# One more fold of the odd rows in a Fourier product: half the columns per product, two row tiles of 128 and 60 rows

## The chip, the cores and the metric

The kernel runs on one core of one Trainium2 chip. The metric is the device time of one launch in microseconds (us). The record lists every run as fast; the program runs on a single core, and no run stood out as slow. In this kernel SBUF holds the tiles that the engines read and write, and PSUM the results of the matmuls.

## The reference, cut to what matters

```python
def _attn_ref(x):                      # x: (8, 3008, 256) float32
    X = np.fft.fft(x, axis=1)          # over the sequence, S = 3008
    X = np.fft.fft(X, axis=2)          # over the features, D = 256
    return X.real.astype(np.float32)

def _moe_ref(x, w_in, w_out):          # w_in (256, 2048), w_out (2048, 256)
    h = x @ w_in
    r = np.maximum(h, 0.0)
    return (r * r @ w_out).astype(np.float32)
```

## The kernel before

TensorE does two things. The **main loop** multiplies the transformed sequence with the first weight (`front`, two products per half step) and the squared result with the second (`back`, seven products per step). The **transform over S** of sequence b + 1 is slipped between the half steps of sequence b as "side work", paced by weights. It is done with tables of cosines and sines. The input is folded first, by symmetry, so that only n from 0 to S/4 = 752 is left. The n are then cut into classes, each with its own small product, and VectorE joins the results. Class 3 holds the 376 odd n, and its products are the ones that the change replaces:

```python
def class_tiles(S):                     # rows (n) by class, at most 128 per tile
    half = S // 8 + 1
    tiles = []
    for c, order in enumerate((range(0, half, 4), range(2, half, 4), range(1, half, 2), range(half, S // 4 + 1))):
        for r in range(0, len(order), P):
            tiles.append((c, order[r], order.step, len(order[r:r + P])))
    return tiles                        # rows: 95 | 94 | 128, 60 | 128, 128, 120

            def product(ps, c):         # one product per row tile of the class
                ts = [t for t in range(NT) if TILES[t][0] == c]
                for t in ts:
                    ...
                    nc.tensor.matmul(ps, w, tab[0:rows, kp, PLACE[t]:PLACE[t] + NC[kp][c]],
                                     start=t == ts[0], stop=t == ts[-1])

            def even_n():               # classes 0, 1 (95 columns) and 2 (189 columns)
                ...
                for c, at, nk in ((0, 0, n2), (1, n2, n2), (2, 2 * n2, n1)):
                    product(st["ps"][:, at:at + nk], c)

            def odd_n():                # class 3, 377 or 376 columns
                st["odd"] = psd.tile([P, 512], F32, name="pd", tag="d")[0:n, 0:n0]
                product(st["odd"], 3)

            def join_1():               # VectorE: even and odd n together
                both(dst[...], dst[...], st["c"], st["odd"])

    def between():                      # called after each half step of the main loop
        nonlocal spent
        if i < 2 * NJ:                  # NJ = 8 steps make one block
            return
        spent -= pace
        while side and spent <= 0:
            t, f = side.pop(0)
            f()
            spent += t
```

There is one such group (even product, odd product, joins) for each parity of k (`kp`) and for cosine and sine (`which`): four per sequence.

Of the kernel before, what the change touches and what calls it, by code (L numbers as in the profile page):

```python
# [8 lines left out]
F32 = mybir.dt.float32  # L9
U32 = mybir.dt.uint32  # L10
AF = mybir.ActivationFunctionType
ALU = mybir.AluOpType
PSUM = bass.MemoryType.PSUM
P = 128
R = 32



# [59 lines left out]
def kernel(  # L78
# [12 lines left out]
    nc = tc.nc  # L91
    B, NROW, _, D = x.shape
    S = out.shape[0] // B
    M = S // 2
    NKT = M + 1
# [14 lines left out]
    const = ctx.enter_context(tc.tile_pool(name="const", bufs=1))  # L110
    xp = ctx.enter_context(tc.tile_pool(name="xp", bufs=NX))
    fp = ctx.enter_context(tc.tile_pool(name="fp", bufs=2))
    wp = ctx.enter_context(tc.tile_pool(name="wp", bufs=NT))
    pq = ctx.enter_context(tc.tile_pool(name="pq", bufs=2))
    hp = ctx.enter_context(tc.tile_pool(name="hp", bufs=3))
    gp = ctx.enter_context(tc.tile_pool(name="gp", bufs=4))
# [11 lines left out]

    xt = {}

    def load_x(b, t):
        _, r0, step, rows = TILES[t]

        while rows % 15 and rows % 16 and r0 + step * rows < NROW:
            rows += 1

        pool, tag = (gp, "g") if b == 0 and t < NT - NX else (xp, "x")
        xt[b, t] = pool.tile([P, 4, D], F32, name="xt", tag=tag)
        nc.sync.dma_start(out=xt[b, t][0:rows], in_=x[b, r0:r0 + step * (rows - 1) + 1:step])
# [121 lines left out]

    folded = {}
    PQE = {}
    NE = B - 1
    xe, we = {}, {}
    e_dram = dp.tile([NE, NKT], F32, name="e_dram")
    e_rows = const.tile([NE, NKT], F32, name="e_rows")

    def load_column(t):

# [14 lines left out]
    def fold(b, t):  # L285


        r = slice(0, TILES[t][3])
        st = {}

        def new(pool, nm, shape):
            st[nm] = pool.tile(shape, F32, name=nm, tag=nm)
            return st[nm]

        def f_s():
            v = xt[b, t]
            tt(out=new(fp, "fs", [P, 2, D])[r], in0=v[r, 0::2], in1=v[r, 1::2], op=ALU.add)

        def f_d():
            v = xt[b, t]  # L300
            tt(out=new(fp, "fd", [P, 2, D])[r], in0=v[r, 0::2], in1=v[r, 1::2], op=ALU.subtract)  # L301
            if b > 0 and b * NT + t + NX < B * NT:
                load_x(*divmod(b * NT + t + NX, NT))

        def f_sc():
            s, sc = st["fs"], new(fp, "sc", [P, 2, H + 1])
            nc.vector.tensor_copy(sc[r, :, 0:H + 1:H], s[r, :, 0:H + 1:H])
            tt(out=sc[r, :, 1:H], in0=s[r, :, 1:H], in1=s[r, :, D - 1:H:-1], op=ALU.add)

        def f_dc():  # L310
            d = st["fd"]
            tt(out=new(fp, "dc", [P, 2, H - 1])[r], in0=d[r, :, 1:H], in1=d[r, :, D - 1:H:-1], op=ALU.subtract)

        def f_p():
            sc, wP = st["sc"], new(wp, "wP", [P, 2, H + 1])
            for kp in range(2):
                tt(out=wP[r, kp], in0=sc[r, 0], in1=sc[r, 1], op=ALU.subtract if kp else ALU.add)
            folded[b, t, 0] = wP

        def f_q():  # L320
            dc, wQ = st["dc"], new(wp, "wQ", [P, 2, H - 1])
            for kp in range(2):
                tt(out=wQ[r, kp], in0=dc[r, 0], in1=dc[r, 1], op=ALU.add if kp else ALU.subtract)
            folded[b, t, 1] = wQ

        return [(0.7, f_s), (0.7, f_d), (0.5, f_sc), (0.4, f_dc), (0.6, f_p), (0.6, f_q)]

    def dft_ops(b):



        def start():
            PQE[b] = [pq.tile([n, NKT], F32, name=nm, tag=nm)
                      for nm, n in (("Pt", P), ("Qt", P - 1), ("Et", P))]

        def group(kp, which):
            n = NE if b is None else P - 1 if which == 1 else P
            tab = sinT if which == 1 else cosT
            n2, _, n1, n0 = NC[kp]
            st = {}  # L340

            def product(ps, c):
                ts = [t for t in range(NT) if TILES[t][0] == c]
                for t in ts:
                    rows = TILES[t][3]
                    w = we[t] if b is None else folded[b, t, which % 2]
                    w = w[0:rows, kp]
                    w = w[:, H:H + 1].to_broadcast([rows, n]) if which == 2 and b is not None else w[:, 0:n]
                    nc.tensor.matmul(ps, w, tab[0:rows, kp, PLACE[t]:PLACE[t] + NC[kp][c]],  # L349
                                     start=t == ts[0], stop=t == ts[-1])  # L350

            def even_n():
                st["ps"] = psd.tile([P, 512], F32, name="pd", tag="d")[0:n]
                a = st["a"] = hp.tile([P, 2 * P], F32, name="da", tag="da", bufs=2)[0:n]
                for c, at, nk in ((0, 0, n2), (1, n2, n2), (2, 2 * n2, n1)):
                    product(st["ps"][:, at:at + nk], c)
                nc.scalar.copy(a[:, 0:n2], st["ps"][:, 0:n2])

            def both(lo, hi, a, ps):

                nk, nh = a.shape[-1], hi.shape[-1]
                tt(out=lo, in0=a, in1=ps, op=ALU.add)  # L362
                if which == 1:
                    tt(out=hi[:, ::-1], in0=ps[:, 0:nh], in1=a[:, 0:nh], op=ALU.subtract)
                else:
                    tt(out=hi[:, ::-1], in0=a[:, 0:nh], in1=ps[:, 0:nh], op=ALU.subtract)

            def join_4():
                a, ps = st["a"], st["ps"]
                st["b"] = hp.tile([P, 2 * P], F32, name="db", tag="db", bufs=2)[0:n, 0:n1]  # L370
                both(st["b"][:, 0:n2], st["b"][:, n2:n1], a[:, 0:n2], ps[:, n2:2 * n2])

            def join_2():
                a, ps = st["b"], st["ps"]
                st["c"] = hp.tile([P, NC[0][3]], F32, name="dc2", tag="dc2", bufs=2)[0:n, 0:n0]
                both(st["c"][:, 0:n1], st["c"][:, n1:n0], a, ps[:, 2 * n2:2 * n2 + n1])

            def odd_n():
                st["odd"] = psd.tile([P, 512], F32, name="pd", tag="d")[0:n, 0:n0]
                product(st["odd"], 3)  # L380

            def join_1():
                dst = e_rows if b is None else PQE[b][which]
                nh = S // 8
                both(dst[:, kp:kp + 2 * n0 - 1:2], dst[:, M - kp - 2 * (nh - 1):M - kp + 1:2], st["c"],
                     st["odd"])

            return [(0.5, even_n), (0.5, join_4), (0.7, join_2), (0.0, odd_n), (1.2, join_1)]

        ops = [] if b is None else [(0.0, start)]  # L390
        for which in (2,) if b is None else (0, 1) if b else (0, 2, 1):
            for kp in range(2):
                ops += group(kp, which)
        if b is None:
            ops.append((0.0, lambda: nc.sync.dma_start(out=e_dram[:, :], in_=e_rows)))
        return ops

    def load_e(b):
# [203 lines left out]
    def between():  # L602

        nonlocal spent
        if i < 2 * NJ:
            return
        spent -= pace
        while side and spent <= 0:
            t, f = side.pop(0)
            f()  # L610
            spent += t

    flight, finished = [], []
    for i in range(len(steps) + LAG + 4):
        if i < len(steps):
            b, k0, n, j = steps[i]
            if i == NJ:
                for t in range(NX):
                    load_x(1, t)
            if NJ <= i < NJ + NT:  # L620
                load_column(i - NJ)
            if i % per == 0:
                assert not side
                side = ahead(b + 1) if b + 1 < B else []
                spent, pace = 0.0, sum(t for t, _ in side) / (2 * (per - (0 if i else 2 * NJ)) - 6)
            g = front(b, k0, n, j, between)
            if i < NJ:
                s = combine(n, g, True)
            elif i < 2 * NJ:
                sum_wout(j)  # L630
        while finished and finished[0][0] <= i:
            store(*finished.pop(0)[1:])
        if i >= LAG and flight:
            at, g_, s_ = flight.pop(0)
            final = at[:3] == (B - 1, *BLOCKS[-1])
            back(at[2], at[3], g_, s_, final)
            if at[3] == NJ - 1:
                c_ = gather(at[2], s_ is None, final)
                finished += [(i + 2 + s, *at[:3], s, c_, final) for s in range(2)]
        for f in products:  # L640
            f()
        products = [next_weight() for _ in range(2 if i + 2 < NJ else 1 if i < NJ else 0)]
        if i < len(steps):
            flight.append(((b, k0, n, j), g, s if i < NJ else combine(n, g, False)))
# [63 lines left out]
```

## Time and profile before

| | before |
|---|---|
| median of 3 runs | 1997.95 us (1997.23 to 2001.38) |
| TensorE busy | 98% of the span |
| VectorE, ScalarE, GpSimd busy | 70%, 45%, 58% |
| odd products of sequences 1 to 7 | 28 x 1.90 us |
| even products of sequences 1 to 7 | 28 x 1.37 us, each with a visit to 60-row weights |

The prediction below shows the lines. In them a matmul in fp32 is two records, PE is the matmul and PEld the weight load, which normally hides under the matmul before it.

### The profile page before, as it was taken

To read this page: it belongs to the slowest core of one execution; us is meant where nothing else is said; L and a number is where in the kernel's file an instruction comes from. 1 tells how busy PE (TensorE), PEld (TensorE's weight loads), DVE (VectorE), ACT (ScalarE), POOL (GpSimd) and SP (SyncE) were. 2 spreads that over 40 slices of the span, in tenths; PEclk is the share of its full clock that TensorE was granted. 3 is DMA by queue.
4 is the path that set the end of the run, shared out by engine and by line. 5 is a ranking of instruction groups with operands and counts; after the bars stand their busy time and mean duration, and the time that the engine had idled before them with its cause. 6 is when DMAs were issued, how large, how long until landed. Compare 5 with 4: busy or idle time off the path is not lost.

```text
span 1999.2 us, 27284 instructions
## 1 busy us (share of the span) xinstructions
PE 1963.1 (98%) x9104; PEld 1704.3 (85%) x9104; DVE 1392.0 (70%) x3492; ACT 897.6 (45%) x973; POOL 1159.3 (58%) x1695
## 2 busy tenths in 40 slices
PE   6899999999999999999999999999999999999998
PEld 3688888888888888888888888888888888888887
DVE  7788866777568765777558875687657776555554
ACT  1654444444444444444445444444444454445443
POOL 0026645666566755676556665666656675566664
PEclk8899999999999999999999999999999999999999
DMA  6232101110011111111011110111001100100100
GB/s 183 95 57 50 38 11 32 47 32 22 11 52 32 27 27 32 26 39 40 11 27 37 39 30 11 31 42 37 21 11 43 41 11 16 31 11 11 22 11 21
DMA packets 144687, 68.49 MB, mean 34 GB/s; under 512 B 128440, under 2 KB 135547, under 8 KB 144546
## 3 DMA queue, kind: packets, MB, share of 16 engines
q1 hardware_dynamic: 143470, 66.24, 14.3%
q8 instruction: 71, 1.16, 0.2%
q10 hardware_dynamic: 1076, 0.52, 0.1%
q14 instruction: 70, 0.57, 0.1%
HBM read 42.03 MB, written 24.68 MB: 33 GB/s over the span
## 4 chain that ended last, share of the span: by engine, by line
PE 94%; DVE 3%; ACT 1%; DMA 1%; issue 0%; SPq 0%; DVEq 0%; ACTq 0%
PE ph L412 16%; PE ph L413 16%; PE mA L465 16%; PE mC L465 16%; PE mB L465 16%; PE mD L465 8%; PE pd L349 5%; DMA xt<-in_x_dram 1%; DVE he L415 0%; PE mA L452 0%; PE mB L452 0%; DVE g L418 0%; PE pg L236 0%; DVE fd L301 0%; ACT g L427 0%
## 5 line engine op out<-in xcount | busy, mean ns | idle before, releaser
L427 ACT ACTIVATE g<-g 128x1004 f32<-128x1004 f32 (+1 forms) x384 | 400.1, 1042 | 896.6 <-DVE g L418 503.6
L415 DVE SCALAR_TENSOR_TENSOR he<-Et,gE,ph 128x251 f32<-128x251 f32 (+1 forms) x768 | 361.8, 471 | 474.9 <-PE ph L413 473.3
L435 POOL TENSOR_TENSOR s<-g 128x251 f32<-128x251 f32 (+1 forms) x376 | 248.6, 661 | 746.5 <-ACT g L428 690.9
L412 PE MATMUL ph<-Pt,G 128*128 128x251 f32 (+1 forms) x1536 | 454.5, 377 | 3.5 <-ACT G L237 2.5
L413 PE MATMUL ph<-Qt,G 127*128 127x251 f32 (+1 forms) x1536 | 452.3, 375 | 0.0
L428 ACT ACTIVATE g<-g 128x1004 f32<-128x1004 f32 (+1 forms) x384 | 399.9, 1041 | 12.2
L465 PE MATMUL mC<-s,wsum 128*128 128x251 f32 (+1 forms) x1504 | 381.3, 374 | 0.0
L465 PE MATMUL mA<-g,wout 128*128 128x251 f32 (+1 forms) x1504 | 380.9, 375 | 0.0
L417 DVE TENSOR_TENSOR g<-he,ph 128x251 f32<-128x251 f32 (+1 forms) x768 | 320.6, 417 | 55.6 <-POOL s L437 0.5
L412 PEld LDWEIGHTS ph<-Pt,G 128*128 128x128 f32 x1536 | 288.0, 189 | 48.0 <-issue 4.5
L413 PEld LDWEIGHTS ph<-Qt,G 127*128 127x128 f32 x1536 | 291.7, 190 | 36.5 <-DVE Qt L362 0.5
L465 PEld LDWEIGHTS mA<-g,wout 128*128 128x128 f32 x1504 | 282.5, 189 | 41.6 <-issue 2.9
L465 PEld LDWEIGHTS mC<-s,wsum 128*128 128x128 f32 x1504 | 285.5, 190 | 34.5
L418 DVE TENSOR_TENSOR g<-he,ph 128x251 f32<-128x251 f32 (+1 forms) x768 | 314.2, 409 | 0.0
L436 POOL TENSOR_TENSOR s<-s,g 128x251 f32<-128x251 f32 (+1 forms) x376 | 282.1, 750 | 29.4
L437 POOL TENSOR_TENSOR s<-g 128x251 f32<-128x251 f32 (+1 forms) x376 | 290.3, 772 | 0.0
L438 POOL TENSOR_TENSOR s<-g,s 128x251 f32<-128x251 f32 (+1 forms) x376 | 247.9, 659 | 0.0
L465 PE MATMUL mB<-g,wsum 128*128 128x251 f32 (+1 forms) x752 | 220.4, 374 | 0.0
L465 PE MATMUL mD<-s,wout 128*128 128x251 f32 (+1 forms) x752 | 220.3, 374 | 0.0
L465 PE MATMUL mB<-s,wout 128*128 128x251 f32 (+1 forms) x752 | 219.9, 374 | 0.0
L465 PEld LDWEIGHTS mB<-g,wsum 128*128 128x128 f32 x752 | 142.6, 190 | 17.4
L465 PEld LDWEIGHTS mD<-s,wout 128*128 128x128 f32 x752 | 141.9, 189 | 17.7
(85 smaller groups left out, 1271.0 us busy)
## 6 DMA issues: line engine op xcount, KB each, us to landing
out_dram<-os SPq DMA_DIRECT2D x376, 56.0 KB
xt<-in_x_dram SPq DMA_DIRECT2D x24, 512.0 KB
xt<-in_x_dram SPq DMA_DIRECT2D x16, 384.0 KB
Et<-e_dram SPq DMA_DIRECT2D x7, 752.5 KB
out_dram<-os SPq DMA_DIRECT2D x288, 6.8 KB
raw<-in_moe_w_in_dram SPq DMA_DIRECT2D x16, 256.0 KB
raw<-in_moe_w_out_dram SPq DMA_DIRECT2D x16, 256.0 KB
xt<-in_x_dram SPq DMA_DIRECT2D x8, 480.0 KB
```

The costliest lines, as they stand in the source:

```text
L412: nc.tensor.matmul(hP, G1[:, fs], pt[:, ks], start=True, stop=True)
L413: nc.tensor.matmul(hQ, G2[:, fs], qt[:, ks], start=True, stop=True)
L415: nc.vector.scalar_tensor_tensor(out=t, in0=et[:, ks], scalar=gE[:, fc:fc + 1], in1=hP, op0=ALU.mult, op1=ALU.add)
L417: tt(out=g[:, h, 0, 0:n], in0=t, in1=hQ, op=ALU.add)
L418: tt(out=g[:, h, 1, 0:n][:, ::-1], in0=t, in1=hQ, op=ALU.subtract)
L427: act(v, v, AF.Relu)
L428: act(v, v, AF.Square)
L435: gt(out=s1, in0=g21, in1=g22, op=ALU.add)
L436: gt(out=s2, in0=s1, in1=g11, op=ALU.subtract)
L437: gt(out=s3, in0=g11, in1=g21, op=ALU.subtract)
L438: gt(out=s4, in0=g12, in1=s2, op=ALU.subtract)
L465: nc.tensor.matmul(acc[nm][:, i, 0:n], w, v[:, 0:n], start=j == 0 and i == 0, stop=j == NJ - 1, skip_group_check=True)
```

## The change

The intent is to halve the columns of the odd products. The odd n from 1 to 751 pair up as n and 752 - n. For even k the sum and the difference of a pair suffice; for odd k a rotation turns the pair into a cosine and a sine transform on the even-k table. So 188 rows are left in place of 376, and each product needs 189 columns instead of 377. In exchange there are two parts per product, and VectorE and ScalarE have to reverse, add and rotate the rows. The core of the diff:

```diff
+    ODD0 = NT - 3
+    HALF = S // 16                      # 188
+    REST = HALF - P                     # 60
...
+        def f_turn():                   # VectorE: reverse the second half of the rows
+            ...
+                nc.vector.stream_shuffle(w, w, REVERSE)
+            nc.scalar.copy(st["f0"][rows], st["v"][rows, 0])
+        def f_even():
+            tt(out=v, in0=a, in1=w, op=ALU.add)
+            tt(out=w, in0=a, in1=w, op=ALU.subtract)
+            sine(spare("f1", "f1"), st["w"], (0, 1))      # ScalarE, two scalings each
+            sine(spare("f2", "f0"), st["v"], (1, 0))
+        def f_odd():
+            ... nc.vector.scalar_tensor_tensor(out=u, in0=u, scalar=turn[rows, 0, i:i + 1], in1=st[nm][rows], ...)
+        return ops + [(0.7, f_turn), (0.9, f_even), (1.0, f_odd)]
...
             def odd_n():
-                st["odd"] = psd.tile([P, 512], F32, name="pd", tag="d")[0:n, 0:n0]
-                product(st["odd"], 3)
+                ps = psd.tile([P, 512], F32, name="pd", tag="d")[0:n]
+                st["odd"] = ps[:, 0:n0]
+                if not b:
+                    return product(ps[:, 0:n0], 3)
+                nq = (n0 + 2) // 2 if kp else (n0 + 1) // 2
+                for part in range(2):
+                    if kp:
+                        tab, o = (cosT, sinT)[part], 0
+                        to = ps[:, part * nq:part * nq + nq]
+                    else:
+                        tab, o = (cosT, sinT)[which], part
+                        to = ps[:, part:n0:2]
+                    other = part != which
+                    for i, (rows, pair) in enumerate(((P, (ODD0, ODD0 + 1)), (REST, (ODD0 + 2, NT)))):
+                        at = PLACE[ODD0 + i]
+                        nc.tensor.matmul(to, folded[b, pair[other]][0:rows, kp, PART[which]][:, 0:n],
+                                         tab[0:rows, 0, at + o:at + NC[0][3]:2], start=i == 0, stop=i == 1)
+                if kp:                   # a ScalarE copy, then VectorE joins the two parts
+                    ...
...
     def between():
-        if i < 2 * NJ:
+        if i < NJ:
             return
-        spent -= pace
+        spent -= pace / 2 if i < 2 * NJ else pace
```

More of the change, by code (lines that the diff above doesn't have):

```diff
@@ L112 @@
     fp = ctx.enter_context(tc.tile_pool(name="fp", bufs=2))
-    wp = ctx.enter_context(tc.tile_pool(name="wp", bufs=NT))
+    wp = ctx.enter_context(tc.tile_pool(name="wp", bufs=NT + 1))
     pq = ctx.enter_context(tc.tile_pool(name="pq", bufs=2))
@@ L129 @@
     xt = {}
-    def load_x(b, t):
-        _, r0, step, rows = TILES[t]
+    ODD0 = NT - 3
+    HALF = S // 16
+    REST = HALF - P
+    ODD = [[(0, 0, P)],
+           [(p, 2 * HALF - p - R, R) for p in range(0, P, R)],
+           [(0, P, H // 2)] + [(H // 2 + p, 2 * HALF - P - p - R, R) for p in range(0, H // 2, R)]]
+    assert H == P and REST <= H // 2 and TILES[ODD0][0] == 3 and TILES[ODD0 + 1][1] == TILES[ODD0][1] + P
+    def load_x(b, t):
+        c, r0, step, rows = TILES[t]
+        if b and c == 3:
+            xt[b, t] = xp.tile([P, 4, D], F32, name="xt", tag="x")
+            for p, first, count in ODD[t - ODD0]:
+                nc.sync.dma_start(out=xt[b, t][p:p + count], in_=x[b, S // 8 + 1 + first:S // 8 + 1 + first + count])
+            return
         while rows % 15 and rows % 16 and r0 + step * rows < NROW:
@@ L263, with make_turn @@
     PQE = {}
+    PART = (slice(0, H + 1), slice(H + 1, D))
+    REVERSE = list(range(R - 1, -1, -1))
+    turn = const.tile([P, 3, 2], F32, name="turn")
+    def make_turn():
+        for i in range(2):
+            for a, tab in enumerate((cosT, sinT, sinT)):
+                nc.scalar.mul(turn[:, a, i:i + 1], tab[:, 1, PLACE[ODD0 + i]:PLACE[ODD0 + i] + 1], -1.0 if a == 2 else 1.0)
     NE = B - 1
@@ L266 @@
     e_dram = dp.tile([NE, NKT], F32, name="e_dram")
-    e_rows = const.tile([NE, NKT], F32, name="e_rows")
     def load_column(t):
@@ L285, in fold @@
     def fold(b, t):
-        r = slice(0, TILES[t][3])
+        odd = b > 0 and t >= ODD0
+        r = slice(0, P if odd else TILES[t][3])
         st = {}
@@ L312, in f_dc, with w_of @@
             tt(out=new(fp, "dc", [P, 2, H - 1])[r], in0=d[r, :, 1:H], in1=d[r, :, D - 1:H:-1], op=ALU.subtract)
+        def w_of(t):
+            if (b, t) not in folded:
+                folded[b, t] = wp.tile([P, 2, D], F32, name="w", tag="w")
+            return folded[b, t]
         def f_p():
-            sc, wP = st["sc"], new(wp, "wP", [P, 2, H + 1])
+            sc, w = st["sc"], w_of(t)
             for kp in range(2):
-                tt(out=wP[r, kp], in0=sc[r, 0], in1=sc[r, 1], op=ALU.subtract if kp else ALU.add)
@@ L318, in f_p @@
-            folded[b, t, 0] = wP
+                tt(out=w[r, kp, PART[0]], in0=sc[r, 0], in1=sc[r, 1], op=ALU.subtract if kp else ALU.add)
         def f_q():
-            dc, wQ = st["dc"], new(wp, "wQ", [P, 2, H - 1])
+            dc, w = st["dc"], w_of(t)
             for kp in range(2):
-                tt(out=wQ[r, kp], in0=dc[r, 0], in1=dc[r, 1], op=ALU.add if kp else ALU.subtract)
-            folded[b, t, 1] = wQ
-        return [(0.7, f_s), (0.7, f_d), (0.5, f_sc), (0.4, f_dc), (0.6, f_p), (0.6, f_q)]
+                tt(out=w[r, kp, PART[1]], in0=dc[r, 0], in1=dc[r, 1], op=ALU.add if kp else ALU.subtract)
@@ new lines, in fold @@
+        ops = [(0.7, f_s), (0.7, f_d), (0.5, f_sc), (0.4, f_dc), (0.6, f_p), (0.6, f_q)]
+        if not odd or t == ODD0:
+            return ops
+        i = t - ODD0 - 1
+        rows = slice(0, TILES[ODD0 + i][3] if i == 0 else REST)
+        def f_turn():
+            w = w_of(t)
+            if i == 0:
+                st["v"], st["w"] = w_of(ODD0), w
+                nc.vector.stream_shuffle(w, w, REVERSE)
+            else:
+                st["v"], st["w"] = w, w_of(NT)
+                nc.vector.stream_shuffle(st["w"][0:H // 2], w[H // 2:P], REVERSE)
+            spare("f0", "f0")
+            nc.scalar.copy(st["f0"][rows], st["v"][rows, 0])
@@ new lines, in spare, with sine @@
+        def spare(nm, tag):
+            st[nm] = fp.tile([P, D], F32, name=nm, tag=tag, bufs=1)
+            return st[nm]
+        def sine(to, src, signs):
+            for part, a in zip(PART, signs):
+                nc.scalar.mul(to[rows, part], src[rows, 1, part], turn[rows, 1 + a, i:i + 1])
+        def f_even():
+            v, w, a = st["v"][rows, 0], st["w"][rows, 0], st["f0"][rows]
+            tt(out=v, in0=a, in1=w, op=ALU.add)
+            tt(out=w, in0=a, in1=w, op=ALU.subtract)
+            sine(spare("f1", "f1"), st["w"], (0, 1))
+            sine(spare("f2", "f0"), st["v"], (1, 0))
@@ L328, in dft_ops @@
+        def f_odd():
+            for nm, u in (("f1", "v"), ("f2", "w")):
+                u = st[u][rows, 1]
+                nc.vector.scalar_tensor_tensor(out=u, in0=u, scalar=turn[rows, 0, i:i + 1], in1=st[nm][rows],
+                                               op0=ALU.mult, op1=ALU.add)
+        return ops + [(0.7, f_turn), (0.9, f_even), (1.0, f_odd)]
     def dft_ops(b):
@@ L345, in product @@
                     rows = TILES[t][3]
-                    w = we[t] if b is None else folded[b, t, which % 2]
-                    w = w[0:rows, kp]
+                    w = (we[t] if b is None else folded[b, t][:, :, PART[which % 2]])[0:rows, kp]
                     w = w[:, H:H + 1].to_broadcast([rows, n]) if which == 2 and b is not None else w[:, 0:n]
@@ L378, in odd_n, with join_odd @@
             def odd_n():
-                st["odd"] = psd.tile([P, 512], F32, name="pd", tag="d")[0:n, 0:n0]
-                product(st["odd"], 3)
+                ps = psd.tile([P, 512], F32, name="pd", tag="d")[0:n]
[8 more added lines that the diff above has]
+                        other = part != which
+                    else:
+                        tab, o = (cosT, sinT)[which], part
+                        to = ps[:, part:n0:2]
+                        other = part != which
+                    for i, (rows, pair) in enumerate(((P, (ODD0, ODD0 + 1)), (REST, (ODD0 + 2, NT)))):
[3 more added lines that the diff above has]
+                if kp:
+                    st["cos"] = hp.tile([P, nq], F32, name="oc", tag="oc", bufs=1)[0:n]
+                    nc.scalar.copy(st["cos"], ps[:, 0:nq])
+                    st["sin"] = ps[:, nq:2 * nq]
+            def join_odd():
+                a, ps = st["cos"], st["sin"]
+                nq = a.shape[-1]
+                st["odd"] = o = hp.tile([P, NC[1][3]], F32, name="do", tag="do", bufs=1)[0:n, 0:n0]
+                tt(out=o[:, 0::2], in0=a[:, 0:nq - 1], in1=ps[:, 0:nq - 1], op=ALU.add)
+                if which == 1:
+                    tt(out=o[:, 1::2], in0=ps[:, 1:nq], in1=a[:, 1:nq], op=ALU.subtract)
+                else:
+                    tt(out=o[:, 1::2], in0=a[:, 1:nq], in1=ps[:, 1:nq], op=ALU.subtract)
             def join_1():
-                dst = e_rows if b is None else PQE[b][which]
+                dst = PQE[1][2][0:n] if b is None else PQE[b][which]
                 nh = S // 8
@@ L386, in join_1 @@
                      st["odd"])
-            return [(0.5, even_n), (0.5, join_4), (0.7, join_2), (0.0, odd_n), (1.2, join_1)]
+            ops = [(0.5, even_n), (0.5, join_4), (0.7, join_2), (0.0, odd_n), (1.2, join_1)]
+            if b and kp:
+                ops.insert(4, (0.7, join_odd))
+            return ops
         ops = [] if b is None else [(0.0, start)]
@@ L394, in dft_ops @@
         if b is None:
-            ops.append((0.0, lambda: nc.sync.dma_start(out=e_dram[:, :], in_=e_rows)))
+            ops.append((0.0, lambda: nc.sync.dma_start(out=e_dram[:, :], in_=PQE[1][2][0:NE])))
         return ops
@@ L621 @@
                 load_column(i - NJ)
+            if i == NJ:
+                make_turn()
             if i % per == 0:
@@ L624 @@
                 side = ahead(b + 1) if b + 1 < B else []
-                spent, pace = 0.0, sum(t for t, _ in side) / (2 * (per - (0 if i else 2 * NJ)) - 6)
+                spent, pace = 0.0, sum(t for t, _ in side) / (2 * per - 6 - (0 if i else 3 * NJ))
             g = front(b, k0, n, j, between)
```

## The prediction

> **What bounds the kernel now.** I read the busy shares first, then the chain that ended last.
>
> ```profile
> span 1999.2 us, 27284 instructions
> PE 1963.1 (98%) x9104; PEld 1704.3 (85%) x9104; DVE 1392.0 (70%) x3492; ACT 897.6 (45%) x973; POOL 1159.3 (58%) x1695
> ...
> PE 94%; DVE 3%; ACT 1%; DMA 1%; issue 0%; SPq 0%; DVEq 0%; ACTq 0%
> ```
>
> TensorE is busy all the time and 94% of the last chain is its own instructions. A busy row alone does not prove a bound, because matmul ends are modelled, so I looked at starts in the timeline. One step of the main loop has 22 matmul records (every fp32 product is two); steps start at 1059.64, 1064.32 and 1068.99 us: 4.67 us, or 212 ns for 251 columns. That is 0.84 ns a column with nothing between. The table of stretches says where another engine could come in (columns: stretch, then PE, PEld, DVE, ACT, POOL busy).
>
> ```profile
> 123.00:161.00 38.00, 38.00 (x180) 33.79 (x179) 31.05 (x84) 17.32 (x18) 18.40 (x28) 1.00 0.43 29
> 161.00:237.00 76.00, 74.98 (x350) 65.11 (x350) 71.21 (x174) 33.90 (x36) 54.64 (x71) 1.00 0.21 55
> 570.00:690.00 120.00, 120.00 (x567) 106.77 (x566) 94.45 (x228) 56.89 (x59) 81.07 (x114) 1.00 0.15 35
> 690.00:808.00 118.00, 118.00 (x550) 101.75 (x549) 73.11 (x190) 50.78 (x56) 67.67 (x103) 1.00 0.11 25
> ```
>
> Steady folding (570 to 690) leaves VectorE 79% busy and no hole in TensorE. In the first sequence VectorE is 94% busy (71.21 of 76) and TensorE loses only 1 us. So what counts is TensorE time, and TensorE time in the small transform products (tile pd), the only matmuls that the change touches. Their stretches in the timeline:
>
> ```profile
> 474.22 1.44 PE L349 MATMUL pd<-cosT,wP 95*128 95x95 f32 x8
> 475.59 1.11 PE L465 MATMUL mA<-g,wout 128*128 128x251 f32 x4
> ...
> 485.05 2.07 PE L349 MATMUL pd<-cosT,wP 128*128 128x377 f32 x6
> 486.95 0.59 PE L465 MATMUL mA<-g,wout 128*128 128x251 f32 x2
> ```
>
> The six records of an odd product hold TensorE from 485.05 to 486.95: 1.90 us, 317 ns for 377 columns, the same 0.84 ns a column. The eight of an even product (four of 95 columns, four of 189) hold it 1.37 us. At 0.84 ns a column the 189s need 4 x 0.159 = 0.64; the 95s follow at the 0.11 us of a weight load, 0.43 together. That makes 1.07, so 0.3 us is unexplained. The weight loads show where it goes:
>
> ```profile
> 474.22 0.64 PEld L349 LDWEIGHTS pd<-cosT,wP 95*128 95x128 f32 x5
> 475.08 0.29 PEld L349 LDWEIGHTS pd<-cosT,wP 60*128 60x128 f32 x2 [0.22 <-issue]
> 475.59 0.51 PEld L465 LDWEIGHTS mA<-g,wout 128*128 128x128 f32 x3 [0.22 <-issue]
> ```
>
> Elsewhere weights are loaded under the matmul before. Here the weights of **60 rows** are not: their load starts at 475.08, together with their matmul, and the same happens on the way back to 128 rows (load and matmul both at 475.59). In single records the last 128-row matmul starts at 474.83, so its 0.159 us of columns end at 474.98; the 60-row load starts 0.09 later and takes 0.107 before columns flow. The way back shows the same two terms. A change between over 64 rows and 60 rows thus costs about 0.09 + 0.107 = **0.20 us**, in and out 0.40. Weights of 120, 95 and 94 rows show none of it.
>
> **What the Trainium skill says.** "TensorEngine Tiling (Array Packing)", Tiling Modes, Key Properties: row tiling has modes of 128, 64 and 32 rows, and changing the mode drains the engine. The trace agrees: 60 rows pay 0.20 us per change, 94 do not. "Advanced Engine Details and Errata", Memory Cachelines, says that a non-contiguous PSUM pattern slows matmuls much, and that SBUF reads want two hits on a 16-byte line. The change writes PSUM with step 2 for even k and reads its tables with step 2. On PSUM the trace speaks against the page: the closing transposes write with step 2, and the last records of four that start at 1990.55 and end with one at 1990.97 are 0.11 us apart for 128 columns, the full 0.84 ns. On the tables no instruction of this trace has step 2; four-byte items at step 2 are just two per line, so I take no penalty. "SBUF — State Buffer", the section on its two sides: a VectorE instruction with two SBUF inputs and a GpSimd instruction exclude each other. The trace agrees: a wP add takes 0.28 us before GpSimd starts (two end in 0.50) and 0.44 in the mean of the run. I price added adds at the contended rate.
>
> **The change part by part.**
>
> 1. *Odd products on TensorE, seven sequences, two parities of k, cosine and sine: 28 groups.* Removed: 6 records of 377 or 376 columns, 1.90 us. Added: 8 records of 189 columns, 8 x 0.159 = 1.27 us. Counted so, the change saves 0.63 x 28 = 17.6 us; I believe this is its intent. But the order is: part 0 with 128 rows, then 60 rows; part 1 with 128 rows, then 60 rows; then the main loop with 128. That is four mode changes per group, where the old product (128, 128, 120 rows) had none: 4 x 0.20 = 0.79 us. New group: 1.27 + 0.79 = 2.06 us, against 1.90. TensorE gets **longer** by 0.16 x 28 = **+4.5 us**. Even products and the column group stay as they are.
>
> 2. *VectorE, per later sequence:* two reversing shuffles of 512 columns, about 0.70 each (estimate from the 448-column transposes, 0.64); four adds of 256 columns at 0.57 (row dc, 254 columns); four multiply-adds at about 0.60; four joins of 189 columns at 0.35 (row dc of the joins): 1.4 + 2.3 + 2.4 + 1.4 = 7.5 us, 53 us in all, 70% to about 72%. The side work is paced by weights: 36.1 units over 90 slots (0.40 each) become 42.7 (0.47). A fold unit costs 5.04 us / 3.5 = 1.44 us of VectorE, so a step of 4.67 us gets 2 x 0.07 x 1.44 = 0.2 us more: folding goes from 79% to about 83%. Nothing waits for that; the first sequence ran at 94% with 1 us lost. I allow +0.5 us over all later sequences.
>
> 3. *ScalarE:* eight scalings of some 128 columns at 0.27, copies of 256 and 189 columns at 0.37 and 0.32 (slope between its 95- and 502-column copies: 0.24 and 0.58): 2.1 + 0.7 + 0.6 = 3.5 us a sequence, 24 us in all, 45% to 46%. VectorE's odd join now waits for a ScalarE copy, twice a sequence, some 0.4 us; the main loop's products have two steps of lead. Nothing on the end path.
>
> 4. *Earlier side work in sequence 0:* the folds of the next sequence start at the second block at half pace. Pace before: 46.1 / 58 = 0.795; after: 52.7 / 66 = 0.80, so the later part keeps its density. In the second block 16 slots x 0.40 x 1.44 = 9.2 us of VectorE come into a stretch with 38.0 - 31.05 = 7 us free. Some 2 us too much, of which TensorE's buffers hide half: +1 us. The first two x tiles land before 120 us, ahead of the first fold, about 124 us.
>
> 5. *The start* (sequence 0) computes as before; P and Q halves share a tile, but TensorE's waits on single pieces of cosT show that regions are tracked, so I expect no new wait. Transfers: seven small ones in place of three for odd x tiles, off the path.
>
> Sum: 1998 + 4.5 + 0.5 + 1 = **2004 us**.
>
> **Rivals.** (a) *The column count decides*: if the mode change cost nothing here, 1998 - 17 + 1.5 = 1982 us. For it speaks only that the new 60-row records might overlap better; against it, all 28 even products of the later sequences, each with a 60-row visit, show the same 1.37 us. (b) *Step 2 table reads are slow*: if they ran at half rate, 8 x 0.159 more per group, +36 us: 2040. For it: the page's line rule is met with no margin. [...]I give it 5%. (c) *VectorE becomes the bound*: dependent shuffles, folds and scalings arrive in bunches and hold back g; a stall of 1 us per later sequence and 3 us in sequence 0 would make 2011 to 2014. For it: the 94% stretch. Against: no TensorE wait at all after 500 us.
>
> **Range and chances.** The single times before spread from 1997 to 2001. With that and 0 to 7 us of stalls, 1997 to 2013. A result in the middle is inside 2% by far; faster by over 2% would need 40 us, more than double the whole column saving; slower by over 2% needs (b) in full.
>
> **What would show it.** Right: pd records grow from 8 + 6 to 8 + 8 per group; an odd product holds TensorE for about 2.06 us with two separate 60-row visits whose weight loads are exposed; TensorE's span grows by 4 to 6 us with hardly any wait. Wrong: an odd product of about 1.3 us (mode change free), or of 3 us and more (step 2 slow); TensorE waits on VectorE's g in folding stretches (c); VectorE far from 1445 us.

## The result, and the profile after

| | before | after |
|---|---|---|
| median | 1998.56 us (4 runs) | 2007.85 us (4 runs, 2007.22 to 2008.60) |
| ratio | | 1.0045, 95% interval 1.0027 to 1.0062 |

A ratio is the mean time of one kernel's fast runs over that of the other's of the same rounds, so it is not quite the ratio of the medians. By the 2% rule the verdict is "same"; the interval shows a small but real loss.

The page of the changed kernel, its span, busy shares and the shares of the last chain:

```profile
span 2005.4 us, 27645 instructions
...
PE 1967.8 (98%) x9160; PEld 1703.4 (85%) x9160; DVE 1446.5 (72%) x3604; ACT 922.5 (46%) x1063; POOL 1160.5 (58%) x1695
...
PE 89%; DVE 6%; ACT 2%; DMA 1%; POOL 1%; issue 1%; SPq 0%; DVEq 0%; ACTq 0%; POOLq 0%
```

VectorE is 54.5 us busier and ScalarE 24.9 us, as worked out. TensorE has 56 records more: two per group, 28 groups. The bound is still TensorE, but VectorE has grown from 3% to 6% of the chain. Where the time went shows in two places.

**First place, the odd product.** The timeline of one of them, matmuls first, then its weight loads (start in us, duration in us, engine, line, tiles, rows x columns, count, idle time before):

```profile
489.69 2.09 PE L465 MATMUL pd<-cosT,w 128*128 128x189 f32 x8
491.71 0.48 PE L516 MATMUL ph<-Pt,G 128*128 128x251 f32 x1
```

```profile
489.48 0.40 PEld L465 LDWEIGHTS pd<-cosT,w 128*128 128x128 f32 x2
490.12 0.29 PEld L465 LDWEIGHTS pd<-cosT,w 60*128 60x128 f32 x2 [0.23 <-issue]
490.65 0.30 PEld L465 LDWEIGHTS pd<-cosT,w 128*128 128x128 f32 x2 [0.23 <-issue]
491.18 0.29 PEld L465 LDWEIGHTS pd<-cosT,w 60*128 60x128 f32 x2 [0.23 <-issue]
491.71 0.30 PEld L516 LDWEIGHTS ph<-Pt,G 128*128 128x128 f32 x2 [0.24 <-issue]
```

The eight records hold TensorE from 489.69 to 491.71, 2.02 us, where the six of before held it 1.90 us. The weight load jumps 128, 60, 128, 60, 128, and before each jump the loader idles 0.23 us: it does not load ahead across the change. The last jump falls on the next record: it is 0.48 us long where its kind has 0.38. So a group costs 2.12 us instead of 1.90. The start of the same product in successive sequences confirms it: a steady sequence takes 238.63 us where it took 237.77, and 0.86 over four groups is 0.215 us each.

**Second place, sequence 0.** TensorE's waits in the stretch from 122 to 240 us, after the change (columns: who <- whom, us in total, times, longest):

```profile
PE ph L516 <- DVE g L522: 3.6, 6, 1.1
PE mA L569 <- ACT sA L585: 0.5, 1, 0.5
```

Before, the whole stretch from 118 to 330 us had one such wait:

```profile
PE ph L412 <- DVE g L418: 0.9, 1, 0.9
```

And the table of stretches of the changed kernel (busy us of PE, PEld, DVE, ACT, POOL):

```profile
123.00:161.00 38.00, 36.89 (x172) 31.89 (x171) 35.36 (x93) 15.78 (x17) 20.85 (x30) 1.00 0.40 36
161.00:237.00 76.00, 72.79 (x336) 61.65 (x334) 69.18 (x167) 36.62 (x45) 51.39 (x71) 1.00 0.16 46
...
570.00:690.00 120.00, 120.00 (x567) 106.79 (x566) 98.20 (x235) 58.94 (x63) 81.68 (x115) 1.00 0.14 36
```

In the first two rows TensorE now has 1.1 and 3.2 us of holes (before: 0 and 1.0), in the third, a steady sequence, none, though VectorE is 82% busy there. From 330 to 1960 us TensorE is busy without a gap in both kernels.

The holes show less than the waits cost. Before the change, the wait of 0.88 us that ends at 223.75 starts the next record 1.04 us late (two records of 0.212 us began at 222.28), because the modelled end of a record overlaps the next one; and the next pair is 0.69 us long where its kind has 0.59, with its weight load exposed. The starts give the whole loss. These are the first records of the second block and of sequence 1, before and then after:

```profile
121.92 0.37 PE L412 MATMUL ph<-Pt,G 128*128 128x251 f32 x1
332.33 0.38 PE L412 MATMUL ph<-Pt,G 128*128 128x251 f32 x1
```

```profile
117.05 0.37 PE L516 MATMUL ph<-Pt,G 128*128 128x251 f32 x1
333.16 0.38 PE L516 MATMUL ph<-Pt,G 128*128 128x251 f32 x1
```

The stretch takes 216.1 us where it took 210.4, 5.7 more. Four odd products are 0.9 of that, so the waits in sequence 0 cost **4.8 us** more than before.

**Why the spans of the traces differ by less than the times.** The two profiled spans differ by 6.2 us, the medians by 9.3. The rows of the granted clock on the two pages, before and then after, point to the reason:

```profile
PEclk8899999999999999999999999999999999999999
```

```profile
PEclk8999999999999999999999999999999999999999
```

The profiled run of the kernel before, at 2000.96 us one of its slower ones, ran its first block at a lower granted clock: from the first record of the main loop to the second block it took 65.7 us against 62.6 us in the changed kernel. Its main loop also began 1.8 us later (56.2 against 54.4 us; the granted clock from 18 to 56 us was 0.74 against 0.82). This comes and goes with the run and not with the kernel: the run with 96 rows below had the same `88` and took 65.6 us. From the second block to the end the two traces differ by 11.1 us: 6.0 for the odd products, 4.8 for sequence 0 and 0.2 at the end; 11.1 - 3.1 - 1.8 is the 6.2. A lower clock at the start is probably also why single times of the kernel before spread over 1996 to 2002, and why the medians differ by less than 11.1; only one of these runs has a trace, so that is not shown. So beside the ratios I compare the periods of steady sequences, which repeat to 0.1 us (one period of e5_late, 0.3 longer, is the exception).

### The profile page after: what moved, and what is told of

It reads as the page before. It is cut to its first block, busy times and chain, and to the rows that moved or that the text cites. A ratio compares the mean times of both kernels' runs of the same rounds, so it can differ in the third digit from the quotient of the medians.

```text
span 2005.4 us, 27645 instructions
## 1 busy us (share of the span) xinstructions
PE 1967.8 (98%) x9160; PEld 1703.4 (85%) x9160; DVE 1446.5 (72%) x3604; ACT 922.5 (46%) x1063; POOL 1160.5 (58%) x1695
## 4 chain that ended last, share of the span: by engine, by line
PE 89%; DVE 6%; ACT 2%; DMA 1%; POOL 1%; issue 1%; SPq 0%; DVEq 0%; ACTq 0%; POOLq 0%
PE ph L516 16%; PE mA L569 15%; PE ph L517 15%; PE mC L569 15%; PE mB L569 15%; PE mD L569 8%; PE pd L465 3%; PE pd L418 3%; DVE he L519 1%; DVE g L522 1%; DVE g L521 1%; DMA xt<-in_x_dram 1%; ACT g L531 1%; ACT g L532 0%; DVE w L349 0%
## 5 line engine op out<-in xcount | busy, mean ns | idle before, releaser
L540 POOL TENSOR_TENSOR s<-s,g 128x251 f32<-128x251 f32 (+1 forms) x376 | 286.4, 762 | 29.5
```

Of the source, the lines that this page charges most:

```text
L540: gt(out=s2, in0=s1, in1=g11, op=ALU.subtract)
```

## The experiments

The theory after the result: (A) each change between the 60-row weights and those of 94 to 128 rows (a "mode change", as the prediction calls it) costs 0.2 us of TensorE, and four of them per odd product eat the whole saving in columns; (B) VectorE's added work makes TensorE wait, in sequence 0 only; (C) the remaining 10 ns per record come from step 2, either of the table read or of the PSUM write. The main rival to (A) is that the added work or the step 2 makes the kernel slower, and mode changes don't matter.

**1. Both 60-row products after both 128-row products (e1_merge).** Only the loop order; the first product alone clears the bank, as in the kernel's own `back`.

```diff
-                for part in range(2):
-                    ...
-                    for i, (rows, pair) in enumerate(((P, ...), (REST, ...))):
-                        nc.tensor.matmul(to, ..., start=i == 0, stop=i == 1)
+                for i, (rows, pair) in enumerate(((P, ...), (REST, ...))):
+                    for part in range(2):
+                        ...
+                        nc.tensor.matmul(to, ..., start=i == 0 and part == 0, stop=i == 1, skip_group_check=True)
```

> The changed kernel with one edit: an odd product runs both 128-row products first and both 60-row products after them, so two changes of the row mode instead of four, with the same eight records, columns, and work on every other engine. Theory (mode changes decide): each odd product, 2.02 us plus 0.10 us exposed in the record after it, gets 0.40 us shorter, 28 x 0.40 = 11 us in all, about 1996.5 us, a ratio to the kernel before of about 0.999. Rival (the added work of VectorE and ScalarE or the step-2 accesses make it slower): those are untouched, so the ratio stays at 1.0045.

Measured: correct, 1997.98 us, ratio to the kernel before 0.9992 (0.9974 to 1.0009). Its weight loads in one odd product:

```profile
489.11 0.74 PEld L464 LDWEIGHTS pd<-cosT,w 128*128 128x128 f32 x4
490.08 0.63 PEld L464 LDWEIGHTS pd<-cosT,w 60*128 60x128 f32 x4 [0.23 <-issue]
490.95 0.30 PEld L516 LDWEIGHTS ph<-Pt,G 128*128 128x128 f32 x2 [0.24 <-DVE g L522]
```

Two idle gaps in place of four, and the product holds TensorE 1.63 us in place of 2.02. A steady sequence takes 237.08 us, 1.55 less than in the changed kernel, 0.39 per group for two changes avoided. The order of eight unchanged products decides; (A) holds and its rival falls. The last gap is put down to VectorE's g, but the same gap stands as "issue" in the other kernel: the releaser is a guess of the profile.

**2. 96 rows instead of 60 (e2_pad).** The rest rows get a table of their own, zero beyond row 60. Three temporary buffers of VectorE go from two to one to make room.

```diff
+    WIDE = 3 * R                                        # 96
+    rest = const.tile([P, 2, NC_ODD], F32, name="rest")
+    nc.gpsimd.memset(rest, 0.0)
+    ... nc.scalar.copy(rest[0:REST, a], tab[0:REST, 0, PLACE[ODD0 + 1]:PLACE[ODD0 + 1] + NC_ODD])
-                    for i, (rows, pair) in enumerate(((P, ...), (REST, ...))):
+                    for i, (rows, pair) in enumerate(((P, ...), (WIDE, ...))):
+                        table = (cosT, sinT)[a][0:rows, 0, PLACE[ODD0] + o:PLACE[ODD0] + NC_ODD:2]
+                        if i:
+                            table = rest[0:rows, a, o::2]
```

> The changed kernel with the 60-row products run over 96 rows, the rows beyond 60 of the table being zero, so no change of the row mode is left in an odd product. Theory: an odd product shrinks to 8 records of about 0.17 us, 1.36 us, against 2.12 us with its exposed end: 28 x 0.76 = 21 us less than the changed kernel, about 1986.5 us, ratio about 0.994. Rival (VectorE work decides): no change, ratio 1.0045. If the penalty came from small weights in general and not from the mode, 96 rows would still pay part of it.

Measured: correct, 1988.32 us, ratio 0.9945 (0.9929 to 0.9961). One odd product in its timeline:

```profile
491.97 0.50 PE L475 MATMUL pd<-cosT,w 128*128 128x189 f32 x2
492.31 0.50 PE L475 MATMUL pd<-rest,w 96*128 96x189 f32 x2
492.65 0.50 PE L475 MATMUL pd<-cosT,w 128*128 128x188 f32 x2
492.98 0.50 PE L475 MATMUL pd<-rest,mirror 96*128 96x188 f32 x2
493.32 0.38 PE L526 MATMUL ph<-Pt,G 128*128 128x251 f32 x1
```

Starts now follow every 0.34 us for two records, 1.35 us for all eight, and the next record is back to 0.38. A steady sequence takes 235.60 us: 3.03 less than in the changed kernel, 0.76 per group, as expected. More rows with the same columns are faster here. No run has between 61 and 93 rows, so where the cost sets in is not shown. The waits of sequence 0 are unchanged (3.6 us on VectorE's g).

**3. A table with step 1 for half the records (e3_contig).** As e2_pad, with `rest` stored de-interleaved.

```diff
-    rest = const.tile([P, 2, NC_ODD], F32, name="rest")
+    rest = [const.tile([P, 2, (NC_ODD + 1 - o) // 2], F32, name=f"rest{o}") for o in range(2)]
...
-                            table = rest[0:rows, a, o::2]
+                            table = rest[o][0:rows, a]
```

> As the run with 96 rows, but the table of the second row tile lies de-interleaved in SBUF, so four of the eight records of an odd product read their moving operand with step 1 instead of 2; the first row tile still reads with step 2. Theory (the table's step costs the 10 ns by which 189-column records exceed 0.16 us): the start-to-start time of the four second-tile records falls from about 170 to 160 ns, the others stay, for even and odd k alike; 28 x 4 x 0.01 = 1.1 us in the total. Rival (the step of the PSUM write costs it): nothing changes, and records of even k only are slow.

Measured: correct, 1987.14 us, ratio 0.9947 (0.9932 to 0.9962); the times of the two cannot tell 1 us, the trace can:

```profile
487.39 0.50 PE L478 MATMUL pd<-cosT,w 128*128 128x189 f32 x2
487.73 0.48 PE L478 MATMUL pd<-rest,w 96*128 96x189 f32 x2
488.05 0.50 PE L478 MATMUL pd<-cosT,w 128*128 128x188 f32 x2
488.39 0.48 PE L478 MATMUL pd<-rest,mirror 96*128 96x188 f32 x2
```

Over all 28 groups the 96-row records follow each other after 161 ns in the mean, where they took 169 with step 2; the 128-row records stay at 169. Even k (whose PSUM write has step 2 in both kernels) and odd k (whose write is dense) gain alike. So the table's step costs 8 ns per 189 columns, and the PSUM step costs nothing that shows.

**4. The kernel before, with 94 + 94 rows (e4_before_94).** No part of the change is in it. It tests (A) where it was read first, in the even products.

```diff
-        for r in range(0, len(order), P):
-            tiles.append((c, order[r], order.step, len(order[r:r + P])))
+        size = P if len(order) % P > P // 2 else -(-len(order) // -(-len(order) // P))
+        for r in range(0, len(order), size):
+            tiles.append((c, order[r], order.step, len(order[r:r + size])))
```

> The kernel before with one edit that has nothing to do with the change: the 188 rows of the third class are cut into 94 + 94 rows instead of 128 + 60, so that no product has 64 rows or fewer. Theory: each even product loses one visit to 60-row weights, 0.29 us inside and 0.11 us after it, 28 x 0.40 = 11 us over the later sequences, and up to 3 us more in sequence 0 and the column product: about 1986 us, ratio about 0.994. Rival (no mode cost): as many records and columns as before, ratio 1.000.

Measured: correct, 1985.04 us, ratio 0.9926 (0.9911 to 0.9941). An even product of it:

```profile
467.78 1.25 PE L350 MATMUL pd<-cosT,wP 95*128 95x95 f32 x8
468.87 0.59 PE L466 MATMUL mA<-g,wout 128*128 128x251 f32 x2
```

It holds TensorE from 467.78 to 468.87, 1.09 us where it was 1.37, and the record after it is no longer stretched. A steady sequence takes 236.22 us, 1.55 less than before, 0.39 per group. One edit of row counts, on a kernel without the change, gains some 11 us: from the second block to the end its trace is 11.0 us shorter than that of the kernel before, and 28 x 0.39 is 10.9. The medians differ by 14.3. Nothing beyond the 28 products shows in that stretch. The other 3 us must lie before it, where the trace of the kernel before has the lower clock (first block 65.7 us, here 62.6); whether they are the clock or the first sequence's own products is not separated.

**5. The side work of sequence 0 starting as late as before (e5_late).**

```diff
-        if i < NJ:
+        if i < 2 * NJ:
             return
-        spent -= pace / 2 if i < 2 * NJ else pace
+        spent -= pace
```

(and the pace divided by the half steps that are left.)

> The changed kernel with the side work of sequence 0 starting at the third block at full pace, as in the kernel before (52.7 units in 58 half steps instead of 66). If the early start itself costs TensorE the 4.3 us of waits for VectorE that its trace shows between 130 and 237 us, the time falls by 2 to 4 us to about 2004.5. If it is the amount of side work, denser pace makes the waits as long or longer: 2007 to 2012 us. I expect the second, about 2009 us.

Measured: correct, 2007.87 us, ratio 1.0051 (1.0036 to 1.0066): the same as the changed kernel. TensorE waits 4.2 us for VectorE's g, where the changed kernel has 3.6 and 0.5 on ScalarE. By the starts, the waits in sequence 0 cost 3.9 us more than before, where they cost 4.8 in the changed kernel; the times do not resolve that difference. So the early start is not what makes TensorE wait, beyond 1 us at most.

**6. The second sequence on the old path (e6_old1).** The condition `b` becomes `b > 1` in the four places that choose the fold, and the side work is placed as in e5_late.

```diff
-        odd = b > 0 and t >= ODD0
+        odd = b > 1 and t >= ODD0
...
-                if not b:
+                if b is None or b < 2:
                     return product(ps[:, 0:n0], 3)
```

> The changed kernel with the second sequence on the old path (fold once more only from the third sequence on) and the side work of sequence 0 placed as before. The added VectorE work then never meets sequence 0. Theory: the waits of TensorE in sequence 0 go back to the 1 us of the kernel before, some 4 us less, and four odd products go back to 1.90 us, 0.9 us less: about 2003 us, ratio 1.002. The remaining 24 groups x 0.215 = 5.2 us stay. Rival (steady sequences also lose time to VectorE): no more than 1 us changes.

Measured: correct, 2002.70 us, ratio 1.0026 (1.0010 to 1.0043). TensorE's waits from 118 to 330 us, and the stretches:

```profile
PE ph L516 <- DVE g L522: 0.9, 1, 0.9
```

```profile
123.00:161.00 38.00, 38.00 (x181) 33.79 (x180) 31.13 (x81) 16.16 (x17) 21.84 (x32) 1.00 0.35 16
161.00:237.00 76.00, 74.97 (x348) 64.69 (x347) 69.25 (x173) 35.63 (x37) 53.77 (x72) 1.00 0.19 55
```

The waits are those of the kernel before, to 0.1 us, while steady sequences stay at 238.63 us. Against e5_late, what is gone is the added work in sequence 0 and four new odd products, so it is this work that TensorE waits for. That separates (B), sequence 0, from (A), all others. Once sequence 0 is over, the added VectorE work costs nothing that these traces show. What remains above the kernel before is 24 groups x 0.215 = 5.2 us, and the medians differ by 5.3.

**7. Everything that helped (e7_best).** 94 + 94 rows in even products, 96 rows and the de-interleaved table in odd ones, the second sequence on the old path.

> All that should help at once: no row mode below 128 anywhere (94 + 94 rows in even products, 96 rows in the second tile of odd products, its table de-interleaved), and the second sequence on the old path. From the kernel before: even products 28 x 0.40 = 11 us and up to 3 us in sequence 0; odd products of six sequences from 1.90 to about 1.32 us, 24 x 0.58 = 14 us: about 1971 us, ratio 0.986. If VectorE's added work binds in the steady sequences once TensorE is shorter, 1 to 5 us less gain.

Measured: correct, 1972.54 us (1971.23 to 1973.33), ratio 0.9871 (0.9857 to 0.9886): 1.3% faster than the kernel before and 1.8% faster than the changed one (1972.54 against 2007.85, from different calls). A steady sequence takes 233.92 us. TensorE waits 1.1 us in sequence 0 and not at all in the steady sequences.

## Why the prediction was right

The time, 2007.85 us, is inside the range of 1997 to 2013 and within 2% as forecast. The point of 2004 was 4 us low. Term by term, as differences to the kernel before, measured in the traces:

| term of the sum | predicted | measured |
|---|---|---|
| odd products, 28 groups | +4.5 (0.16 each) | +6.0 (0.215 each, from the sequence period) |
| VectorE in later sequences | +0.5 | 0 (no TensorE wait from 330 to 1960 us) |
| sequence 0 | +1 | +4.8 (from the starts; listed waits 4.1 us against 0.9) |
| sum | +6 | +10.8, and +11.1 from the second block to the end; medians +9.3 |

So the terms were 5 us too low, and the point came within 4 us because the medians differ by less than the traces do. That part is luck, whatever the reason.

- **Mode changes (part 1): right, and shown twice over.** Removing two of four changes gave 0.39 us per group, all four 0.76, and one visit less in the kernel before 0.39; the estimate was 0.20 per change. The column saving came nearly as counted: without changes an odd product is 1.32 to 1.35 us (counted: 1.27) against 1.90.
- **The size of the odd product: too small by 0.05 us** (2.06 counted; 2.12 measured with the stretched record after it). The prediction said of the tables with step 2, "I take no penalty". That term was mis-sized: e3_contig shows 8 ns for each 189-column record with step 2, 0.06 us for eight.
- **Step 2 into PSUM: right.** The page's warning did not come true, as the closing transposes had suggested.
- **VectorE's and ScalarE's sums: right** (53 and 24 us predicted, 54.5 and 24.9 measured), although single terms were off: the adds of 256 columns took 0.77 us in the mean, not 0.57, ScalarE's scalings 0.39, not 0.27; the joins were as predicted. The prediction states the exclusion of VectorE and GpSimd too widely: "SBUF — State Buffer" limits it to a GpSimd instruction that reads SBUF, as those of the main loop do. The wP adds that it prices from have a median of 0.29 us and a mean of 0.44. Lines of the changed kernel:

```profile
L386 DVE TENSOR_TENSOR w<-f,w 128x256 f32<-128x256 f32 (+1 forms) x14 | 10.9, 779 | 0.5
L371 DVE STREAM_SHUFFLE w<-w 64x512 f32<-64x512 f32 x7 | 5.1, 731 | 0.2
```

- **Sequence 0: the right cause, the wrong size.** The prediction let "TensorE's buffers hide half" of 2 us, and 4.8 us came. It looked only at the second block, where TensorE now has 1.1 us of holes. Another 3.2 us lie between 161 and 237 us (before: 1.0), where the text said that the density stays. Experiments 5 and 6 show that TensorE waits for the added work. Why the waits are this long stays open. VectorE is not busier in that stretch (69.2 us of 76, before 71.2), and per unit of weight the new pieces are not dearer than the old: two adds, a shuffle and two multiply-adds take 3.4 us for 2.6 units, 1.3 each, where a fold has 1.44. How the pieces bunch, and what they wait for, no run separates.
- **Rival (a), columns decide:** out, as said. **Rival (b), step 2 at half rate:** out; the penalty is 5%. **Rival (c), VectorE becomes the bound:** it foresaw 3 us in sequence 0, where 4.8 came, and 1 us per later sequence, which did not come.

## What to carry to other kernels

Before counting saved columns, write down the row count of every product in the order in which TensorE runs them: a lone tile of 60 rows between tiles of 94 to 128 costs 0.4 us per visit here, as much as some 480 columns of one record. Split 188 rows as 94 + 94, or pad the rest with zero rows to 96, or put the small tiles next to each other. Where an engine is already full, a sum of busy times does not tell what added side work costs: read it from the starts of the bound engine's records. And compare traces stage by stage, since a lower clock at the start can hide some us.

## What the Trainium skill lacked or had wrong

- "TensorEngine Tiling (Array Packing)", Tiling Modes, Key Properties, says that a change of mode drains the engine, but gives no cost and not that a plain product of 60 rows in the middle of 128-row products pays it. Measured: about 0.20 us per change in fp32 (estimated as 0.09 us before the weight load and 0.107 us of load that is no longer hidden); 94, 95, 96 and 120 rows pay nothing. That the tiling mode is the reason fits, and no run tests it apart from the row count.
- "Advanced Engine Details and Errata", Memory Cachelines, PSUM: any pattern that isn't contiguous is said to slow matmuls significantly. Measured: with fp32 products and step 2, nothing (the odd products of even k, which write with step 2, and of odd k, which write densely, both take 1.35 us in e2_pad).
- The same section, SBUF: accesses that hit the same line are said to run at full speed, and two hits are the least that absorbs the latency. Measured: a moving operand of four-byte items at step 2, two per line, takes 169 ns for 189 columns where step 1 takes 161, 5% more.
